# Fused sliding-window attention and MoE block: the last head pair of batches 3 to 7 returned to x^T by the transposing DMA, and seven MoE units in slots 13 to 15

## The chip, the core and the metric

The kernel runs on one core of one Trainium2 chip. The metric is the device time of one execution in microseconds, and smaller is better. Three runs of the kernel before gave 325.88, 325.59 and 325.86 us; their median is 325.86 us.

## The reference: what is computed

Attention over q, k, v of 8 batches, 8 heads, 576 tokens and 64 elements, with a causal window of 128 tokens and a bias that falls linearly with distance (ALiBi). Its output, with the heads side by side, is x of 4608 tokens by 512. Behind it stands a two-layer block with a hard-swish between the layers:

```python
scores = scale * q @ k^T + slope[h] * -(|i - j|)      # only 0 <= i - j < 128
attn   = softmax(scores)
x      = (attn @ v) with heads side by side            # 4608 x 512
h      = x @ w_in                                      # 512 -> 2048
g      = h * clip(h + 3, 0, 6) / 6
out    = g @ w_out                                     # 2048 -> 512, float32
```

## The kernel before, in words

**Tiles.** Attention goes by *head pairs*: pair g holds two heads of batch g // 4, so there are 32 of them, and pairs 3, 7, ..., 31 are the last of their batch. The block goes by tiles nt of 512 tokens, 9 of them. For each tile there are 16 units "U" (`moe_up`: four matmuls of 128x512 over the four 128-row slices ks of x^T, in the order ks = 0 to 3, then a ScalarE activation L470 and a VectorE product L471) and 16 units "D" (`moe_down`: four matmuls of 128x512, L501; after every fourth D, VectorE copies the result (L510) and SyncE sends it out (L511)). Slice ks of x^T is what head pair ks of a batch has put there: the last pair of a batch writes slice 3.

**x^T.** It lies in the tile `xT`, a ring of four batches of 576 columns and 64 columns behind them. `back(g)` (L421) takes the normalized attention output of a pair (`avs`, 128 tokens by 5 groups by 128) and puts its transpose there in one of two ways. Where `by_xbar(g)` (L418) is true, SyncE issues one transposing DMA (L425) of 640 columns. Else TensorE does five 128x128 transposes (L432) into a PSUM bank of the pool that the U units use too, and ScalarE copies 576 columns (L438).

**Order of the work.** From batch 2 on, `segment` (L669) writes out by hand the order of every engine's queue, in slots g = 8 to 32. In slot g come: the scores of pair g (L296, L322, L328), the exps of g on ScalarE and their masks on GpSimd (L351, L354, L361, L364, L367, L370), and, on the results of the slot before, the products with v of pair g - 1 in two halves (`values`: first three groups, then two; L383, L391), each followed by a VectorE reciprocal and product that write `avs` (L401, L402). Between these pieces `fill(n)` puts n MoE units into the queues. The seven numbers `f` say how many go where: `FILLS` gives (1, 1, 1, 2, 0, 1, 1) for slots 9, 10 and 11, which is seven units in a slot, and all others take (1, 1, 1, 2, 0, 1, 2), which is eight. `back(g - 1)` stands behind the second half of `values` where it goes by DMA, and at the slot's end, ahead of its last unit, where it goes by TensorE.

**The order of the units** is one fixed list of 288 (`ORDER`, L513). `fill` stops short where the next unit is a U whose tokens are not all in `xT` yet (L528): `done` counts the pairs that have been put back. With the DMA it rises at the start of the next slot but one (L672), with TensorE at once. What is left of the list when the slots end is put into the queues without a break (`fill(len(units))`, L733); I call that the tail.

**SyncE's queue** is in order. In `stage_next` (L540) it gets, for the batches ahead, the loads of q, k and v (five DMAs each, L112) and the transposing DMAs of q and k (L199) out of one buffer `tbuf`, into which GpSimd casts first q and then k (L194). In slots 16, 20 and 24 `stage_next` comes behind `back` and issues the loads of k and the transposing DMA of q for the next batch; one slot later follow v and the transposing DMA of k. The output DMAs (L511) go through the same queue.

Of the kernel before, what the change touches and what calls it, by code (L numbers as in the profile page):

```python
# [18 lines left out]
def kernel(  # L19
# [16 lines left out]
    NP = H // 2  # L36
# [11 lines left out]
    XB = 2 * NP  # L48
# [367 lines left out]
    done = [0]  # L416

    def by_xbar(g):  # L418
        return g >= XB and g % NP < NP - 1 and g != XB + 2

    def back(g):  # L421
        b, hp = divmod(g, NP)
        avs = st[g, "avs"].rearrange("p j e d -> p j (e d)")
        if by_xbar(g):
            nc.sync.dma_start_transpose(  # L425
                out=xT[:, hp, ds(b % 4 * S, SP)].rearrange("p (j c) -> p j c", j=NQ),
                in_=avs.rearrange("p j c -> p (j c)"))
            return
        pool, tag = (ps_o, "o") if b < 2 else (ps_h, "h")
        tp = pool.tile([128, SP], BF16, tag=tag, name="tb", padded_shape=[128, 1024])  # L430
        for j in range(NQ):
            nc.tensor.transpose(tp[:, ts(j, 128)], avs[:, j, :], ident)  # L432
        if g == NP - 1:
            nc.scalar.copy(out=xT[:, hp, ds(b % 4 * S, 256)], in_=tp[:, 0:256])
            nc.vector.tensor_copy(out=xT[:, hp, ds(b % 4 * S + 256, S - 256)], in_=tp[:, 256:S])
            return
        eng = nc.vector.tensor_copy if g == 2 * NP - 1 else nc.scalar.copy
        eng(out=xT[:, hp, ds(b % 4 * S, S)], in_=tp[:, 0:S])  # L438
# [84 lines left out]
    def fill(n):  # L523
        for _ in range(n):
            if at[0] == len(units):
                return
            nt, fn, step = units[at[0]]
            if fn is moe_up and done[0] < NP * (min((nt * NT + NT - 1) // S, B - 1) + 1):  # L528
                return
            fn(nt if fn is moe_up else nt - 1, step)  # L530
            at[0] += 1
# [132 lines left out]
        scores_diag(2 * NP)  # L664
        scores_off(2 * NP)

    FILLS = {g: (1, 1, 1, 2, 0, 1, 1) for g in (9, 10, 11)}

    def segment(lo, hi, fills):  # L669
        for g in range(lo, hi + 1):  # L670
            f = fills(g)
            if by_xbar(g - 2):  # L672
                done[0] = g - 1
            if lo < g < hi and g != 3 * NP + 1:
                scores(g)
            turn = {2 * NP: (2, 1, "k"), 2 * NP + 1: (2, 1, "q"),
                    2 * NP + 2: (3, 0, "k"), 2 * NP + 3: (3, 1, "k")}.get(g)
            if turn:
                double(*turn, 0, "av", A)
            fill(f[0])  # L680
            if turn:
                double(*turn, 1, *(("h", V) if turn[0] == 2 else ("av", A)))
            if g < hi:
                exp_diag(g, 0)
            fill(f[1])
            if g < hi:
                exp_diag(g, 1)
            if g == 3 * NP:
                cast_tokens(3, "v")
            if g > lo:  # L690
                values(g - 1, (0, 1, 2))
            fill(f[2])
            if g < hi:
                exp_off(g, 0)
            fill(f[3])
            if g < hi:
                exp_off(g, 1)
            if g > lo:
                values(g - 1, (3, 4))
            fill(f[4])  # L700
            if g > lo and by_xbar(g - 1):
                back(g - 1)
            fill(f[5])
            if g < hi:
                stage_next(g)
            fill(1)
            if g == 3 * NP:
                scores(g + 1)
            if g > lo and not by_xbar(g - 1):
                back(g - 1)  # L710
                done[0] = g
            fill(f[6] - 1)
# [3 lines left out]
    with tc.manual_schedule(engines=every):  # L716
# [13 lines left out]
        fill(2)  # L730
        segment(2 * NP, G, lambda g: FILLS.get(g, (1, 1, 1, 2, 0, 1, 2)))
        done[0] = G
# [31 lines left out]
```

## Time and profile before

| what | value |
|---|---|
| median of three runs | 325.86 us |
| span of the profiled execution | 325.3 us |
| TensorE busy | 314.0 us (97%) |
| ScalarE busy | 198.4 us (61%) |
| VectorE busy | 173.7 us (53%) |
| GpSimd busy | 141.4 us (43%) |
| matmuls of U (L451) and D (L501) | 146.2 and 138.6 us |
| transposes of `back` on TensorE (L432) | 75 in 15 pairs |
| transposing DMAs into `xT` (L425) | 17 |

The span runs from the first to the last instruction of the one profiled execution; what lies around it in a run's time is the half microsecond to the median. In a timeline row the first number is the start in us from the span's start and the second the duration; then come the engine, the line, the operation and the tiles, and in brackets the idle time of the engine ahead of it with what ended it. A matmul's duration counts until the model's end of its pipeline, so two that follow each other overlap in the rows; distances from start to start tell more.

### The profile page before, as it was taken

How to read it: one execution, taken by the hardware profiler on the slowest of the kernel's cores; microseconds unless marked ns; L12 is line 12 of the kernel's file. 1: busy time of each engine (PE TensorE's matmuls, PEld its weight loads, DVE VectorE, ACT ScalarE, POOL GpSimd, SP SyncE). 2: the span in 40 equal slices, each digit the busy share in tenths (PEclk: the TensorE clock that was granted, in tenths of full speed). 3: DMA queues.
4: the chain of work that ended last, by engine and by line, in shares of the span. 5: the costliest groups of instructions: out<-in, count | busy, mean ns of one | idle time of the engine just before them, and what ended most of it. 6: DMA issues, size and time to landing. Idle time of an engine off the chain costs nothing.

```text
span 325.3 us, 7087 instructions
## 1 busy us (share of the span) xinstructions
PE 314.0 (97%) x2763; PEld 168.4 (52%) x2763; DVE 173.7 (53%) x338; ACT 198.4 (61%) x339; POOL 141.4 (43%) x249
## 2 busy tenths in 40 slices
PE   7869999999999999999999999999999999999996
PEld 6555465455555555555667655554554444444443
DVE  7657565554445655565555555554565544445510
ACT  4748877877766666666666666666666344244411
POOL 7446393495395566636663666462342000000000
PEclk9999999999999999999999999999999999999999
DMA  7999999799999999799989986931114100000112
GB/s 274 197 328 180 224 298 191 167 257 218 202 254 176 238 212 208 178 222 217 194 146 229 198 207 138 202 107 64 40 36 55 64 33 34 32 32 34 61 41 91
DMA packets 128065, 51.08 MB, mean 157 GB/s; under 512 B 115616, under 2 KB 119968, under 8 KB 128032
## 3 DMA queue, kind: packets, MB, share of 16 engines
q1 hardware_dynamic: 122800, 44.54, 63.4%
q0 software_dynamic: 4224, 4.19, 8.2%
q10 hardware_dynamic: 1008, 1.90, 1.6%
q8 instruction: 21, 0.34, 0.5%
q14 instruction: 12, 0.10, 0.1%
HBM read 36.70 MB, written 9.44 MB: 142 GB/s over the span
## 4 chain that ended last, share of the span: by engine, by line
PE 82%; DMA 7%; ACT 4%; SPq 3%; DVE 1%; issue 1%; POOL 0%; ACTq 0%
PE ops L501 37%; PE hps L451 34%; DMA ldbuf<-in_q_dram 3%; PE scd L296 2%; PE av L391 2%; DMA w_in_sb<-in_moe_w_in_dram 2%; SPq L112 2%; PE av L383 2%; DMA ldbuf<-in_k_dram 2%; ACT r L470 2%; SPq L98 1%; PE sco L328 1%; ACT xT L438 1%; PE ops L482 1%; PE tb L432 1%
## 5 line engine op out<-in xcount | busy, mean ns | idle before, releaser
L471 DVE SCALAR_TENSOR_TENSOR gbuf<-r,hps 128x512 bf16<-128x512 f32 x144 | 98.5, 686 | 104.8 <-ACT r L470 104.8
L470 ACT ACTIVATE r<-hps,bias 128x512 f32<-128x512 f32 x144 | 99.0, 689 | 82.1 <-PE hps L451 81.8
L451 PE MATMUL hps<-xT,w_in_sb 128*128 128x512 bf16 (+1 forms) x640 | 146.2, 358 | 2.7 <-DMA w_in_sb<-in_moe_w_in_dram 1.9
L501 PE MATMUL ops<-w_out_sb,gbuf 128*128 128x512 bf16 x560 | 138.6, 379 | 0.0
L451 PEld LDWEIGHTS <-w_in_sb 128*128 128x128 bf16 x640 | 58.8, 98 | 56.4 <-DMA w_in_sb<-in_moe_w_in_dram 3.0
L501 PEld LDWEIGHTS <-gbuf 128*128 128x128 bf16 x560 | 52.0, 98 | 56.0
L354 POOL TENSOR_SCALAR_AFFINE_SELECT pd<-pd 128x512 bf16<-128x512 bf16 x48 | 30.0, 633 | 58.4 <-ACT pd L351 58.4
L364 POOL TENSOR_SCALAR_AFFINE_SELECT po<-po 128x512 bf16<-128x512 bf16 x48 | 30.3, 634 | 25.5 <-ACT po L361 24.7
L351 ACT ACTIVATE pd<-scd,bias_d 128x512 bf16<-128x512 f32 x48 | 32.1, 685 | 2.6 <-POOL vbuf L187 2.6
L361 ACT ACTIVATE po<-sco,bias_o 128x512 bf16<-128x512 f32 x48 | 33.2, 692 | 0.0
L510 DVE COPY osb<-ops 128x512 f32<-128x512 f32 x33 | 22.7, 688 | 18.7 <-PE ops L501 18.1
L194 POOL CAST tbuf<-ldbuf 128x512 bf16<-128x512 f32 (+1 forms) x45 | 25.6, 611 | 3.9 <-DMA qTb<-tbuf 3.1
L402 DVE TENSOR_TENSOR avs<-av,rc 128x384 bf16<-128x384 f32 (+1 forms) x48 | 23.6, 491 | 1.6
L391 PEld LDWEIGHTS <-pd 128*128 128x128 bf16 x192 | 14.3, 97 | 8.2 <-issue 0.9
L438 ACT COPY xT<-tb 128x576 bf16<-128x576 bf16 x13 | 8.3, 638 | 16.7 <-PE tb L432 16.7
L383 PE MATMUL av<-vbuf,po 128*128 128x65 bf16 x192 | 18.0, 193 | 0.0
L391 PE MATMUL av<-vbuf,pd 128*128 128x65 bf16 x192 | 17.3, 194 | 0.3 <-ACT kTb L244 0.3
L187 POOL CAST vbuf<-ldbuf 128x1024 bf16<-128x1024 f32 x14 | 14.3, 1040 | 5.2 <-DMA ldbuf<-in_v_dram 5.2
L383 PEld LDWEIGHTS <-po 128*128 128x128 bf16 x192 | 14.3, 98 | 3.0 <-DVE avs L402 0.5
L227 POOL CAST pr<-ldbuf 128x576 bf16<-128x576 f32 x20 | 12.8, 668 | 6.6 <-PE tb L432 2.5
L367 ACT ACTIVATE p4buf<-sco,bias_d 128x64 bf16<-128x64 f32 x48 | 15.7, 327 | 0.0
L296 PEld LDWEIGHTS <-kTb 64*128 64x128 bf16 x256 | 7.2, 94 | 14.1 <-issue 10.6
(96 smaller groups left out, 227.3 us busy)
## 6 DMA issues: line engine op xcount, KB each, us to landing
out_dram<-osb SPq DMA_DIRECT2D x33, 256.0 KB, 2.4
ldbuf<-in_v_dram SPq DMA_DIRECT2D x32, 256.0 KB, 5.6
ldbuf<-in_q_dram SPq DMA_DIRECT2D x20, 256.0 KB, 4.7
ldbuf<-in_k_dram SPq DMA_DIRECT2D x16, 256.0 KB, 4.8
ldbuf<-in_q_dram SPq DMA_DIRECT2D x12, 288.0 KB, 7.8
ldbuf<-in_k_dram SPq DMA_DIRECT2D x12, 288.0 KB, 8.1
w_in_sb<-in_moe_w_in_dram POOLq DMA_DIRECT2D x4, 512.0 KB, 9.8
w_out_sb<-in_moe_w_out_dram POOLq DMA_DIRECT2D x4, 512.0 KB, 11.3
```

The lines of the kernel that those rows point to most:

```text
L194: nc.gpsimd.tensor_copy(out=tbuf[:m, :, j, :], in_=s[:m, j, :, :].rearrange("p (i e) d -> p i (e d)", e=2))
L351: nc.scalar.activation(out=pd[:, e, :, :].rearrange("p j c -> p (j c)"), in_=sc[:, e, :], func=ACT.Exp, bias=bias_d[:, h:h + 1], scale=scale)
L354: nc.gpsimd.affine_select(out=pd[:, e, :, :], in_=pd[:, e, :, :], pattern=[[0, 4], [1, 128]], channel_multiplier=-1, base=0, compare_op=AL ...
L361: nc.scalar.activation(out=po[:, e, :, :].rearrange("p j c -> p (j c)"), in_=sc[:, e, :], func=ACT.Exp, bias=bias_o[:, h:h + 1], scale=scale)
L364: nc.gpsimd.affine_select(out=po[:, e, :, :], in_=po[:, e, :, :], pattern=[[0, 4], [-1, 128]], channel_multiplier=1, base=-1, compare_op=A ...
L383: nc.tensor.matmul(out_av, lhsT=po[:, e, qt % 4, :], rhs=vb[:, qt - 1, h, :], start=True, stop=False)
L391: nc.tensor.matmul(out_av, lhsT=d, rhs=vb[:, qt, h, :], start=(qt == 0), stop=True)
L402: nc.vector.tensor_tensor(out=st[g, "avs"][:, qts[0]:qts[0] + nq, :, :], in0=av[:, 0:nq, :, 0:D], in1=rc[:, 0:nq, :, :].to_broadcast([128, ...
L451: nc.tensor.matmul(hps[:, lo:hi], lhsT=w_in_sb[:, ks, ts(ms, 128)], rhs=xT[:, ks, ds(src, hi - lo)], start=(ks == 0), stop=(ks == n_ks - 1))
L470: nc.scalar.activation(out=r6, in_=hps, func=ACT.Relu, bias=bias3[:, 0:1], scale=1.0 / 6.0)
L471: nc.vector.scalar_tensor_tensor(out=gts[nt][:, ms, :], in0=r6, scalar=1.0, in1=hps, op0=ALU.min, op1=ALU.mult)
L501: nc.tensor.matmul(ops[nt, sub], lhsT=gts[nt][:, ms, ts(sub, 128)], rhs=w_out_sb[:, ms, :], start=(ms == 0), stop=(ms == n_ms - 1))
```

## The change

```diff
     def by_xbar(g):
-        return g >= XB and g % NP < NP - 1 and g != XB + 2
+        return g >= XB and g != XB + 2 and g != XB + 3
...
-    FILLS = {g: (1, 1, 1, 2, 0, 1, 1) for g in (9, 10, 11)}
+    FILLS = {g: (1, 1, 1, 2, 0, 1, 1) for g in (9, 10, 11, 13, 14, 15)}
```

XB is 8 and NP is 4. Pairs 15, 19, 23, 27 and 31 now go back by the transposing DMA; pairs 10 and 11 stay on TensorE. Slots 13, 14 and 15 take seven units in place of eight. Nothing else changes in the text of the kernel; the list of units is the same, so each of its units behind slot 13 comes up to three places later against the attention.

## The prediction

> **What bounds the kernel now.** I read the page's first part, the clock row and the shares of the chain that ended last.
>
> ```profile
> PE 314.0 (97%) x2763; PEld 168.4 (52%) x2763; DVE 173.7 (53%) x338; ACT 198.4 (61%) x339; POOL 141.4 (43%) x249
> PEclk9999999999999999999999999999999999999999
> PE 82%; DMA 7%; ACT 4%; SPq 3%; DVE 1%; issue 1%; POOL 0%; ACTq 0%
> ```
>
> TensorE is busy for 97% of the span at its full granted clock, and the chain runs on it for 82%; the DMA's 7% belong to the start. So the next view is busy time by stretches: two ordinary slots of eight units, and most of the tail.
>
> ```profile
> 109.50:117.61 8.11, 8.11 (x71) 4.07 (x70) 4.57 (x10) 6.05 (x11) 3.30 (x6) 1.00 1.09 229
> 126.24:134.36 8.12, 8.12 (x69) 4.07 (x70) 3.97 (x9) 6.15 (x11) 3.84 (x8) 1.00 1.14 196
> 257.00:320.00 63.00, 62.92 (x294) 28.67 (x293) 27.16 (x40) 23.34 (x35) 0.00 (x0) 1.00 0.11 42
> ```
>
> The columns behind the length are TensorE, weight loads, VectorE, ScalarE, GpSimd, clock, DMA share (over 1 here) and GB/s. An ordinary slot is TensorE from end to end, 8.11 us of 8.11; ScalarE has about 2 us to spare. The tail is as dense. What leaves TensorE's queue therefore shortens the time by its own length, as long as nothing else comes late.
>
> Now the slots that hold a `back` on TensorE. This is TensorE's timeline; the L296 rows are the starts of the slots' scores, and the slots are 16 (117.61), 20, 24, 28 and 32.
>
> ```profile
> 117.61 0.40 PE L296 MATMUL scd<-qTb,kTb 64*128 64x128 bf16 x8
> ...
> 122.79 0.19 PE L383 MATMUL av<-vbuf,po 128*128 128x65 bf16 x1
> ...
> 124.76 0.44 PE L432 MATMUL tb<-ident,avs 128*128 128x128 bf16 x5
> 125.04 1.27 PE L451 MATMUL hps<-xT,w_in_sb 128*128 128x512 bf16 x4
> 126.24 0.40 PE L296 MATMUL scd<-qTb,kTb 64*128 64x128 bf16 x8
> ...
> 150.58 0.40 PE L296 MATMUL scd<-qTb,kTb 64*128 64x128 bf16 x8
> ...
> 159.11 0.40 PE L296 MATMUL scd<-qTb,kTb 64*128 64x128 bf16 x8
> ...
> 183.58 0.40 PE L296 MATMUL scd<-qTb,kTb 64*128 64x128 bf16 x8
> ...
> 192.24 0.40 PE L296 MATMUL scd<-qTb,kTb 64*128 64x128 bf16 x8
> ...
> 216.57 0.40 PE L296 MATMUL scd<-qTb,kTb 64*128 64x128 bf16 x8
> ...
> 225.21 0.40 PE L296 MATMUL scd<-qTb,kTb 64*128 64x128 bf16 x8
> ...
> 256.05 0.44 PE L432 MATMUL tb<-ident,avs 128*128 128x128 bf16 x5
> 256.33 2.13 PE L451 MATMUL hps<-xT,w_in_sb 128*128 128x512 bf16 x8
> 258.29 1.03 PE L501 MATMUL ops<-w_out_sb,gbuf 128*128 128x512 bf16 x4
> ```
>
> From scores to scores these slots take 8.63, 8.53, 8.66 and 8.64 us, with eight units each like the ordinary 8.12. The excess is 0.51, 0.41, 0.54 and 0.52 us. It has two parts. The five transposes take 0.28 us (124.76 to 125.04). The U behind them is the first of the next tile, and its last matmul reads the slice that has just been transposed:
>
> ```profile
> 125.24 0.64 ACT L438 COPY xT<-tb 128x576 bf16<-128x576 bf16 x1 [1.73 <-PE tb L432]
> ```
>
> ScalarE's copy ends at 125.88, but the fourth matmul would have been due three quarters of a unit behind 125.04. A unit's length comes from the chain's longest piece:
>
> ```profile
> 308.53 10.36 PE ops L501 x48
> ```
>
> Forty-eight matmuls are twelve units, so 0.863 us each, and the fourth matmul was due at 125.69. So TensorE waits there, which is the rest of the excess, some 0.24 us.
>
> **The change part by part.**
>
> *Five backs leave TensorE and ScalarE.* In slots 16, 20, 24 and 28 the excess goes: 0.51 + 0.41 + 0.54 + 0.52 = 1.98 us. In slot 32 the transposes take 256.33 - 256.05 = 0.28 us, and the two U behind take 258.29 - 256.33 = 1.96 in place of 1.73, another 0.23; together 0.51. In all 2.49 us. The five copies on ScalarE (0.64 each) lie beside TensorE and are worth nothing beyond the wait just counted. The PSUM bank that `tb` took is free for U units; I give that nothing, as no wait for that bank shows in an ordinary slot.
>
> *Three units move to the tail.* Slots 13 to 15 lose 3 x 0.863 = 2.59 us of TensorE work and the tail gets it back: 78 units in place of 75. Both are TensorE from end to end, so the sum is nothing. The cover is that a seven-unit slot stays bound by TensorE: 8.11 - 0.86 = 7.25 us against 6.05 us or less on ScalarE, 4.57 on VectorE and 3.30 on GpSimd in the ordinary slot. If these slots did not shrink at all, the change would cost 2.59 here. Counted through the list, no `fill` from slot 16 on is cut short: the first U of a new tile now falls to the third `fill` of slots 17, 21, 25, 29, where `done` has risen, and in the tail to the third unit. That is what the shift by three units does.
>
> *Five transposing DMAs are added.* Each has to land ahead of the fourth matmul of that U. The time from `avs` and the time to landing:
>
> ```profile
> 123.46 0.42 DVE L402 TENSOR_TENSOR avs<-av,rc 128x256 bf16<-128x256 f32 x1
> ```
>
> ```profile
> DMA to landing us min/median/max: 2.4/2.7/4.9
> ```
>
> The second half of `values` starts at 122.79 and `avs` is complete at 123.88, that is 1.09 us later. TensorE's time from the start of that half to that U in the next slot is five units (three here, two there) and all the attention of a slot, 8.12 - 8 x 0.863 = 1.21 us: 5.53 us, and 0.65 more to its fourth matmul, 6.18. The DMA of the shown 17 needs 1.09 + 2.4 to 4.9 = 3.5 to 6.0 us. In the tail there are five units and the half itself (0.25) ahead, and 0.65: 5.22 against the same 3.5 to 6.0. So at the median (3.8) nothing waits, with 2.4 and 1.4 us in hand; at the longest landing slot 32 would lose 0.8. I take zero, nearest to the median, and keep up to 1 us for the range.
>
> *SyncE waits at a new place.* The added DMA stands ahead of the loads of k in slots 16, 20 and 24, and waits there for `avs`; behind it wait five loads, the transposing DMA of q and the outputs. For them GpSimd's cast of k waits (it needs `tbuf` free), and in the end the scores of the next batch.
>
> ```profile
> 108.28 3.72 SPq L199 DMA_TRANSPOSE kTb<-tbuf  x1
> ...
> 121.92 5.38 SPq L112 DMA_DIRECT2D ldbuf<-in_k_dram  x5
> ...
> 139.30 3.73 SPq L199 DMA_TRANSPOSE kTb<-tbuf  x1
> ...
> 153.47 4.56 SPq L112 DMA_DIRECT2D ldbuf<-in_k_dram  x5
> ...
> 185.93 0.38 SPq L511 DMA_DIRECT2D out_dram<-osb  x1
> 186.36 5.36 SPq L112 DMA_DIRECT2D ldbuf<-in_k_dram  x5
> ```
>
> ```profile
> DMA to landing us min/median/max: 4.9/5.5/7.0
> ```
>
> Capacity first: the twelve groups of issues from 153.47 to 185.93 come to 27.8 us in a period of 32.9 (to 186.36). One more L425 of about 1.24 makes 29.1 of the new 32.4. It fits, with less to spare.
>
> Then the deadlines. Batch 4: k's transposing DMA is issued at 108.28, which the change does not move, and lands at 113.8 (115.3 at the longest). The scores of pair 16 come at 117.61 - 2.59 = 115.0. Batch 5: `avs` of pair 15 is complete at 123.88 - 2.59 = 121.3, SyncE is free at 121.9, so the loads of k start 1.25 us later than before, and k's DMA goes out at 139.30 + 1.25 = 140.6 at the latest, landing at 146.1 (147.6). The scores of pair 20 are due at 150.58 - 2.59 - 0.51 = 147.5. Both hold at the median by over a microsecond and miss by 0.1 to 0.3 at the longest landing. From batch 6 on, SyncE waits for `avs` itself: the loads start at 156.86 - 3.1 + 1.25 = 155.0 in place of 153.47 and end at 159.6; q's DMA lands by 166.6 at the longest, and then GpSimd casts k:
>
> ```profile
> 166.69 2.83 POOL L194 CAST tbuf<-ldbuf 128x512 bf16<-128x512 f32 x5
> 170.24 0.64 POOL L354 TENSOR_SCALAR_AFFINE_SELECT pd<-pd 128x512 bf16<-128x512 bf16 x1 [0.72 <-ACT pd L351]
> ```
>
> The cast then ends at 169.4, and the four large masks of pair 22 behind it (0.6 each) at 171.9. They are needed by the first `values` of slot 23, at 159.11 - 3.5 + 2 x 8.12 + 2.3 = 174.2. It holds by 2 us. I take zero for this step, and up to 1.5 us for the range.
>
> The sum is -2.49 us. The span is 325.3 us and the median of the runs 325.86, half a microsecond around it, so I take the sum from the median: 325.86 - 2.49 = 323.4 us.
>
> **The rivals.**
>
> *The transposing DMA lands behind the U that needs it (slower).* The place is the fourth matmul of the first U of tiles 3 to 7. With a landing of T the loss is 4 x (T + 1.09 - 6.18) + (T + 1.09 - 5.22) = 5 T - 24.5 us; from T = 5.4 us it is more than the 2.49 gained. At T = 7.0, the longest landing of the larger q and k transposes, it is 10.5 us, so 333.9 us. For it speaks that the new DMAs run beside output and load traffic, where the longest of the 17 was measured; against it, that all 17 stay below 5.4. Chance 0.07.
>
> The Trainium skill speaks for this rival: VectorE: DVE Perf Modes, in "The three transpose paths", gives 1309 ns for a 128x128 transpose by DMA against 390 ns on TensorE, and its "Rules for kernel authors" take TensorE where a PSUM destination will do. Taken one after another, five such blocks make 6.5 us by my estimate from that page, and the sum would be 331.6 us. The trace disagrees for this shape: the five blocks land in 2.4 to 4.9 us together, and five on TensorE take 0.28 us of its queue.
>
> *SyncE's queue makes the q and k transposes late (part of the gain lost).* For it: the two margins above that vanish at the longest landings. Against it: even the full shift of the loads (5 us against TensorE's work) meets 5.8 us (batch 5: 139.30 + 5.5 to 150.58) in hand. A loss of 0.3 us up to 0.5 in each of four batches gives 324.4, between 323.7 and 325.4. Chance 0.12.
>
> *The seven-unit slots do not shrink, or a fill runs dry (no change).* The three units then cost 2.59 us in the tail and eat the gain: 325.9 us. For it: SyncE issues without a gap through these slots. Against it: no engine but TensorE is near full in them. Chance 0.07.
>
> **How the numbers follow.** The forecast, 323.4 us with its own range 322.9 to 323.8, has 0.74. The measurement tells 0.2% (0.65 us) from no change, so faster is anything under 325.2. Faster: 0.74 and most of the second rival, 0.84. Same: the third and the rest of the second, 0.08. Slower: 0.08. The range reaches from 322.8, if the two parts of the excess are a little larger than counted, to 324.8, which takes in the bounds of late landing and two thirds of the second rival.
>
> **What would show it.** Right: slots 16, 20, 24 and 28 take 8.1 us from scores to scores, slots 13 to 15 about 7.25, no L432 behind 93 us, 22 DMAs of L425, and TensorE without a wait at the first U of tiles 3 to 7. Wrong: TensorE idle ahead of a U with the DMA into `xT` as releaser; idle ahead of the scores of pairs 16, 20, 24 or 28 with qTb or kTb as releaser; GpSimd's masks behind a longer wait for `tbuf` and `values` waiting for them.

## The result, and the profile after

| | before | after | ratio, 95% interval |
|---|---|---|---|
| first measurement, 4 runs each | 325.87 us | 322.97 us | 0.9918 [0.9903, 0.9932] |
| second, 35 and 12 runs | 325.91 us | 324.26 us | 0.9946 [0.9925, 0.9967] |
| third, 23 and 12 runs | 326.28 us | 323.66 us | 0.9932 [0.9911, 0.9953] |

The changed kernel is faster by 0.5 to 0.8%, that is 1.7 to 2.9 us; 2.5 us were forecast. The three measurements differ by more than such runs should if only the change counted, and the profiles show why: the start of the kernel scatters (below). From the scores in slot 12 on, the traces repeat to a hundredth, so they answer the question of the sum better than the medians.

TensorE's timeline of the changed kernel: the starts of the scores of slots 12 (pair 13), 14, 15, 16, 17, then 20 and 21, 24 and 25, 28 and 29, and between them the U at which the changed kernel could have waited, the first of tile 3.

```profile
90.22 0.40 PE L296 MATMUL scd<-qTb,kTb 64*128 64x128 bf16 x8
...
99.09 0.40 PE L296 MATMUL scd<-qTb,kTb 64*128 64x128 bf16 x8
...
106.34 0.40 PE L296 MATMUL scd<-qTb,kTb 64*128 64x128 bf16 x8
...
113.58 0.40 PE L296 MATMUL scd<-qTb,kTb 64*128 64x128 bf16 x8
...
121.70 0.40 PE L296 MATMUL scd<-qTb,kTb 64*128 64x128 bf16 x8
...
124.30 1.89 PE L451 MATMUL hps<-xT,w_in_sb 128*128 128x512 bf16 x8
126.03 1.03 PE L501 MATMUL ops<-w_out_sb,gbuf 128*128 128x512 bf16 x4
...
146.04 0.40 PE L296 MATMUL scd<-qTb,kTb 64*128 64x128 bf16 x8
...
154.16 0.40 PE L296 MATMUL scd<-qTb,kTb 64*128 64x128 bf16 x8
...
178.63 0.40 PE L296 MATMUL scd<-qTb,kTb 64*128 64x128 bf16 x8
...
186.78 0.40 PE L296 MATMUL scd<-qTb,kTb 64*128 64x128 bf16 x8
...
211.11 0.40 PE L296 MATMUL scd<-qTb,kTb 64*128 64x128 bf16 x8
...
219.23 0.40 PE L296 MATMUL scd<-qTb,kTb 64*128 64x128 bf16 x8
```

The slots that held a transpose took 8.63, 8.53, 8.66 and 8.64 us; they now take 8.12, 8.12, 8.15 and 8.12, the length of any other. Slots 14 and 15 take 7.25 and 7.24, seven units without a gap. The two U at 124.30 end 1.73 us later to the hundredth: no wait for the new DMA. Now the whole stretch, from the scores in slot 12 to the last output's issue; SyncE's timeline, first of before, then of after:

```profile
322.74 0.33 SPq L486 DMA_DIRECT2D out_dram<-osb  x1
```

```profile
318.83 0.33 SPq L486 DMA_DIRECT2D out_dram<-osb  x1
```

Those scores started at 91.64 us before and at 90.22 after. So the stretch took 322.74 - 91.64 = 231.10 us and takes 318.83 - 90.22 = 228.61 us: 2.49 less, which is the predicted sum. A second profile of before gave 322.03 - 90.93 = 231.10, two more of after 321.88 - 93.26 = 228.62 and 318.42 - 89.80 = 228.62.

What SyncE's queue does around the first new DMA, with the time to landing of all 22, and where GpSimd pays for it:

```profile
119.86 0.53 SPq L511 DMA_DIRECT2D out_dram<-osb  x1
120.96 1.20 SPq L425 DMA_TRANSPOSE xT<-avs  x1
122.21 4.49 SPq L112 DMA_DIRECT2D ldbuf<-in_k_dram  x5
126.81 3.76 SPq L199 DMA_TRANSPOSE qTb<-tbuf  x1
...
138.32 3.73 SPq L199 DMA_TRANSPOSE kTb<-tbuf  x1
```

```profile
DMA to landing us min/median/max: 2.4/2.5/4.3
```

```profile
134.17 2.84 POOL L194 CAST tbuf<-ldbuf 128x512 bf16<-128x512 f32 x5 [5.23 <-DMA qTb<-tbuf]
136.96 1.22 POOL L354 TENSOR_SCALAR_AFFINE_SELECT pd<-pd 128x512 bf16<-128x512 bf16 x2
138.14 1.22 POOL L364 TENSOR_SCALAR_AFFINE_SELECT po<-po 128x512 bf16<-128x512 bf16 x2
```

The loads of k now stand behind the wait for `avs`, and GpSimd waits 5.23 us for `tbuf`. Its masks for pair 18 end at 139.36, and the first products that read them start in slot 19 some 2.3 us behind its scores (137.93), at 140.2. The wait is real, and there was room for it. The room is smaller one batch earlier, in slot 15, where pair 14's masks follow the cast of k for batch 4; GpSimd's timeline, then the first TensorE product that reads a mask of L364:

```profile
103.24 2.84 POOL L194 CAST tbuf<-ldbuf 128x512 bf16<-128x512 f32 x5 [3.80 <-DMA qTb<-tbuf]
...
107.22 1.22 POOL L364 TENSOR_SCALAR_AFFINE_SELECT po<-po 128x512 bf16<-128x512 bf16 x2
```

```profile
108.69 0.19 PE L383 MATMUL av<-vbuf,po 128*128 128x65 bf16 x1
```

These masks end at 108.44, so 0.25 us were in hand; the other two profiles of the changed kernel had 2.25 and 0.4. In the kernel before, the same masks ended at 108.9 and were read at 111.85, 3.0 us later. Counted from the scores in slot 12, the shorter slots bring the reader 1.7 us forward, and q's DMA ahead of that cast landed 7.5 us after its issue in this profile (5.2 and 6.9 in the other two, 5.7 before).

### The profile page after: what moved, and what is told of

It reads as the page before. It is cut to its first block, busy times and chain, and to the rows that moved or that the text cites. A ratio compares the mean times of both kernels' runs of the same rounds, so it can differ in the third digit from the quotient of the medians.

```text
span 321.6 us, 7050 instructions
## 1 busy us (share of the span) xinstructions
PE 312.4 (97%) x2738; PEld 167.6 (52%) x2738; DVE 173.0 (54%) x338; ACT 195.6 (61%) x334; POOL 141.1 (44%) x249
## 4 chain that ended last, share of the span: by engine, by line
PE 82%; DMA 10%; SPq 2%; POOL 2%; DVE 1%; ACT 1%; issue 1%; POOLq 0%
PE ops L501 37%; PE hps L451 33%; DMA w_out_sb<-in_moe_w_out_dram 5%; DMA ldbuf<-in_v_dram 3%; PE scd L296 3%; DMA ldbuf<-in_k_dram 2%; PE av L391 2%; SPq L112 2%; PE av L383 2%; PE sco L328 1%; PE ops L482 1%; PE w L153 1%; POOL w_out_sb L171 1%; PE tp L219 0%; ACT kTb L244 0%
## 5 line engine op out<-in xcount | busy, mean ns | idle before, releaser
L471 DVE SCALAR_TENSOR_TENSOR gbuf<-r,hps 128x512 bf16<-128x512 f32 x144 | 98.7, 687 | 102.5 <-ACT r L470 100.2
L364 POOL TENSOR_SCALAR_AFFINE_SELECT po<-po 128x512 bf16<-128x512 bf16 x48 | 30.3, 636 | 32.5 <-ACT po L361 32.3
L391 PE MATMUL av<-vbuf,pd 128*128 128x65 bf16 x192 | 17.3, 194 | 0.3 <-ACT kTb L244 0.3
L296 PE MATMUL scd<-qTb,kTb 64*128 64x128 bf16 x256 | 12.7, 219 | 1.7 <-DVE kTb L220 0.9
```

What stands on the lines that cost most here:

```text
L296: nc.tensor.matmul(scd[:, e, ts(j, 128)], lhsT=kT[r, j, :], rhs=qT[r, j, :], start=first, stop=first or j == 3)
L364: nc.gpsimd.affine_select(out=po[:, e, :, :], in_=po[:, e, :, :], pattern=[[0, 4], [-1, 128]], channel_multiplier=1, base=-1, compare_op=A ...
L391: nc.tensor.matmul(out_av, lhsT=d, rhs=vb[:, qt, h, :], start=(qt == 0), stop=True)
L471: nc.vector.scalar_tensor_tensor(out=gts[nt][:, ms, :], in0=r6, scalar=1.0, in1=hps, op0=ALU.min, op1=ALU.mult)
```

## The experiments

My theory at this point: the gain is time that leaves TensorE's queue (five transposes and five waits for ScalarE's copy); the moved units are neutral; the DMAs land in time. Rivals: the shift of the units does the work, the landing or SyncE's queue takes part of the gain back, or the change moves the start of the kernel. "Stretch" is the time from the scores in slot 12 to the last output's issue (231.10 before, 228.61 after), taken from each run's trace.

### The five DMAs alone

```diff
-    FILLS = {g: (1, 1, 1, 2, 0, 1, 1) for g in (9, 10, 11, 13, 14, 15)}
+    FILLS = {g: (1, 1, 1, 2, 0, 1, 1) for g in (9, 10, 11)}
```

> The five DMAs alone: slots 13 to 15 keep eight units. Theory (the gain is TensorE's queue time, 5 x 0.28 us of transposes and 5 x 0.23 us of waits for ScalarE's copy; the new DMAs land 2.4 to 2.6 us after their issue): the first U of tile 3 now stands first in slot 17, behind one unit less in slot 16, and its fourth matmul is due 3.3 us behind the second half of values, against 1.09 + 2.4 to 2.6 = 3.5 to 3.7 for the DMA; in slots 21, 25 and 29 it is due after 4.1, in the tail after 3.5. So at most 0.6 us is lost against the changed kernel: 323.0 to 323.6 us. Rival (the landing is what the three moved units are there to cover, at up to 4.9 us): waits of 2.7 + 3 x 1.9 + 2.5 = 10.9 us, up to 333.9 us.

Measured: 325.01 us, 0.9965 [0.9945, 0.9984] of before, where 323.0 to 323.6 was expected; the changed kernel beside it took 324.26. Its stretch is 319.67 - 90.08 = 229.59 us, so 0.98 more than with the shift; 0.6 at most was expected. TensorE's timeline at the first U of tile 3:

```profile
123.29 0.40 PE L296 MATMUL scd<-qTb,kTb 64*128 64x128 bf16 x8
...
123.84 0.82 PE L451 MATMUL hps<-xT,w_in_sb 128*128 128x512 bf16 x3
124.89 1.24 PE L451 MATMUL hps<-xT,w_in_sb 128*128 128x512 bf16 x5 [0.23 <-DMA xT<-avs]
```

Three matmuls run, then the fourth waits for the DMA into its slice, as the theory says; that slot takes 8.50 us in place of 8.12. Slots 25 and 29 take 8.32 and 8.21, and the first two U of tile 7 take 2.02 us in place of 1.73. I had nothing for the two slots and 0.2 us at most for tile 7. For these three, `avs` was complete 1.8, 1.8 and 1.3 us behind the start of the second half of `values`, where I took 1.09 from one slot of the kernel before. So the landing is a real deadline, the DMAs bring 1.5 us by themselves, and three moved units are what buys the last 1.0.

### The seven-unit slots alone

```diff
-    FILLS = {g: (1, 1, 1, 2, 0, 1, 1) for g in (9, 10, 11)}
+    FILLS = {g: (1, 1, 1, 2, 0, 1, 1) for g in (9, 10, 11, 13, 14, 15)}
```

(in the kernel before)

> The seven-unit slots alone: all five last pairs stay on TensorE. Theory: moving three units costs nothing, but the unit behind the transposes is now a D, so the 0.23 us that the first U waited for ScalarE's copy go five times: 325.87 - 1.15 = 324.7 us, with the five transposes of 0.28 us still there. If the wait were only hidden by the DMA and not by the order of units, or if the transposes were the whole excess: 325.9. If the slots did not shrink: 325.9 + 2.6 - 1.15 = 327.3.

Measured: 325.40 us, 0.998 [0.9961, 0.9998]; stretch 320.13 - 89.69 = 230.44, which is 0.66 less than before and not 1.15. TensorE's timeline at the transposes of slot 16:

```profile
119.36 1.03 PE L501 MATMUL ops<-w_out_sb,gbuf 128*128 128x512 bf16 x4
120.22 0.53 PE L432 MATMUL tb<-ident,avs 128*128 128x128 bf16 x5
120.59 1.03 PE L501 MATMUL ops<-w_out_sb,gbuf 128*128 128x512 bf16 x4
121.55 0.40 PE L296 MATMUL scd<-qTb,kTb 64*128 64x128 bf16 x8
```

Behind the transposes stands a D that waits for no copy, and still it starts 0.37 us after them, not 0.28. The excess of the slot is 8.49 - 8.12 = 0.37. VectorE's timeline of this run, then TensorE's weight loads for the transposes in the kernel before and in this run (a transpose loads its 128x128 of `avs` as weights), and the last two loads of this run alone:

```profile
119.17 0.69 DVE L471 SCALAR_TENSOR_TENSOR gbuf<-r,hps 128x512 bf16<-128x512 f32 x1 [0.89 <-ACT r L470]
...
119.98 0.42 DVE L402 TENSOR_TENSOR avs<-av,rc 128x256 bf16<-128x256 f32 x1
```

```profile
124.55 0.48 PEld L432 LDWEIGHTS <-avs 128*128 128x128 bf16 x5
```

```profile
120.01 0.57 PEld L432 LDWEIGHTS <-avs 128*128 128x128 bf16 x5
```

```profile
120.46 0.11 PEld L432 LDWEIGHTS <-avs 128*128 128x128 bf16 x2
```

The five loads take 0.09 us longer, and that is a new wait. The fourth transpose is the first that reads the second half of `avs`. Here this half is complete at 120.41, behind the start of the transposes, and the fourth load starts at 120.46; in the kernel before it was complete at 123.88, 0.9 us ahead of the transposes. The three moved units put a U in place of a D just ahead of the second half of `values`, and VectorE makes that U's product (L471, to 119.86) before it turns to `avs`. So this run takes the waits for the copy away and puts five smaller waits for `avs` in.

### The transposes kept, without use

```diff
+            elif g > lo and g % NP == 0:
+                avs = st[g - 1, "avs"].rearrange("p j e d -> p j (e d)")
+                tp = ps_h.tile([128, SP], BF16, tag="h", name="tb", padded_shape=[128, 1024])
+                for j in range(NQ):
+                    nc.tensor.transpose(tp[:, ts(j, 128)], avs[:, j, :], ident)
```

(in the changed kernel, where `back` by TensorE stood)

> The changed kernel, and beside the five DMAs the five transposes of the last pairs on TensorE as before, at the same place, but with no copy and no reader: work that is left without use, to price the transposes alone. Theory: 5 x 0.28 = 1.4 us more than the changed kernel, 324.4 us, and no wait at the U behind them. If the PSUM bank they take makes U units wait: more than 1.4. If TensorE had room for them: 323.0.

Measured: 325.63 us, 0.9985 [0.9968, 1.0002] of before; stretch 320.92 - 90.47 = 230.45, so 1.84 us more than the changed kernel: five times 0.37, where five times 0.28 was expected. TensorE had no room for them. TensorE's weight loads in slot 16:

```profile
120.79 0.57 PEld L716 LDWEIGHTS <-avs 128*128 128x128 bf16 x5
```

They take 0.57 us as in the run before it, with the same wait of the fourth for `avs` (complete at 121.19, loaded at 121.24), so with 5 x 0.28 = 1.4 us and some 0.4 of such waits nothing is left for a wait for the PSUM bank. The two runs agree from both sides: 0.66 by the order of units and 1.84 by the transposes are 2.50, the whole of the gain. The waits for `avs` make the first number smaller and the second larger by as much.

### The DMA behind the loads of k

```diff
-            if g > lo and by_xbar(g - 1):
+            if g > lo and by_xbar(g - 1) and g % NP:
                 back(g - 1)
             fill(f[5])
             if g < hi:
                 stage_next(g)
+            if g > lo and by_xbar(g - 1) and g % NP == 0:
+                back(g - 1)
             fill(1)
```

> The changed kernel with the last pair's DMA issued behind the loads of k and the transposing DMA of q in slots 16, 20 and 24 (in 28 and 32 nothing stands ahead of it), so that SyncE does not wait for avs ahead of the loads. Theory of the deadline: in slot 16 SyncE is free at 121.0, the loads take 4.5 to 5.4 us and q's DMA 3.8, so the DMA into xT goes out near 130.3 and lands near 132.9, against the fourth matmul of the first U of tile 3 due near 125.0: a wait of 6 to 8 us, three times, so 18 to 24 us: 341 to 347 us. TensorE idle at that U with the DMA into xT as releaser. Rival (the order on SyncE matters little, or the loads that come earlier give time back): under 330.

Measured: 348.19 us, 1.0674 [1.0644, 1.0705], above the 341 to 347 expected. TensorE's timeline at the first U of tile 3, and the stretch of slot 17 cut in five (TensorE busy is the second number, the clock the third from the end):

```profile
130.98 2.29 PE L451 MATMUL hps<-xT,w_in_sb 128*128 128x512 bf16 x5 [6.46 <-DMA xT<-avs]
```

```profile
121.11:124.50 3.39, 3.23 (x39) 1.87 (x40) 0.90 (x4) 1.26 (x2) 3.39 (x7) 1.00 1.18 244
124.52:129.18 4.66, 0.00 (x1) 0.00 (x0) 0.47 (x1) 0.00 (x0) 0.03 (x1) 1.00 1.36 215
129.22:130.98 1.76, 0.00 (x0) 0.00 (x0) 0.00 (x0) 0.00 (x0) 0.00 (x0) 0.50 0.65 155
130.98:136.05 5.07, 5.07 (x19) 2.06 (x19) 1.93 (x4) 2.94 (x6) 2.04 (x5) 0.50 0.11 43
136.05:138.32 2.27, 2.27 (x13) 0.89 (x11) 0.73 (x2) 0.69 (x1) 2.25 (x5) 1.00 0.32 72
```

The mechanism of the prediction's slower rival is there where it was put. Its price was too low: the slot grew by 17.21 - 8.12 = 9.1 us, of which 6.5 are the wait. The rest is the clock: it falls to 0.50 while TensorE idles, and when TensorE starts again it stays there for 5.1 us, which costs half of them. Three such slots (17, 21 and 25: waits of 17.3 us together) cost the stretch 343.95 - 89.62 - 228.61 = 25.7 us. So a late landing costs about 1.5 times its wait here, once the wait is this long. The Trainium skill, in TensorE: Matmul & The Clock Gate, "The HAM clock gate (the "warmup" mystery)", has the gate fall to half rate after an idle window of about 3.4 us and come back after a busy one of that length, and the window is free-running. This run agrees on the half rate. The fall came 4.7 us into the idling and the return 5.1 us into the work; both are longer than one window, which a free-running window allows.

### Pair 10 by the DMA too

```diff
-        return g >= XB and g != XB + 2 and g != XB + 3
+        return g >= XB and g != XB + 3
```

> The changed kernel with pair 10 back by the DMA too (pair 11 stays). Theory: in slot 11 five more transposes leave TensorE, 0.28 us, at most 0.37 with the gap up to the scores behind them, and the first U that needs pair 10 comes a slot later: 322.6 to 322.7 us. Rival (SyncE's queue is full around slot 12 and the added issue makes q and k late): 323.0 or more.

Measured: 323.78 us, 0.9938 [0.9917, 0.9959] of before; 322.6 to 322.7 was expected. Slot 11 is 0.29 us shorter (8.21 for 8.50), as expected, but slot 13 is 0.79 longer (9.66 for 8.87). SyncE's timeline, then TensorE's:

```profile
82.58 4.17 SPq L112 DMA_DIRECT2D ldbuf<-in_q_dram  x5
86.85 0.56 SPq L511 DMA_DIRECT2D out_dram<-osb  x1
87.50 1.91 SPq L425 DMA_TRANSPOSE xT<-avs  x1
```

```profile
91.90 1.46 PE L451 MATMUL hps<-xT,w_in_sb 128*128 128x512 bf16 x6 [0.86 <-DMA xT<-avs]
```

`avs` of pair 10 was complete at 84.38, but SyncE was busy issuing loads; the DMA went out at 87.50, landed at 91.9, and the first U of tile 2 waited 0.86 us. By the trace that loses 0.5 us in all, where I expected a gain of 0.3 (from the scores in slot 9 to the last output's issue 257.57 us, and 257.10 in the changed kernel); the medians can't tell it from the changed kernel. It is not the rival either: TensorE waited nowhere for q or k, but for the added DMA itself. My expectation had the next U "a slot later", but slot 12, whose fills are cut short, takes only 4.0 us.

### Pair 10 by the DMA, and the loads of q behind it

```diff
-    LOADS = {9: "v3", 10: "q4", 12: "k4", 13: "v4", 14: "q5", 16: "k5", 17: "v5", 18: "q6",
+    LOADS = {9: "v3", 11: "q4", 12: "k4", 13: "v4", 14: "q5", 16: "k5", 17: "v5", 18: "q6",
```

(on top of the run before)

> Pair 10 back by the DMA as in the run that did so alone, and the loads of q for batch 4 moved one slot later, behind that DMA on SyncE. In the run with pair 10 alone the DMA of pair 10 stood behind those loads (82.58 to 86.75) and an output, went out at 87.50 though avs was complete at 84.4, landed 4.4 us later, and TensorE waited 0.86 us for it at the first U of tile 2. Theory: with the loads behind it the DMA goes out near 84.5 and that wait goes, so from the scores of slot 9 to the last output the trace shows 257.1 - 0.3 = 256.8 us, 0.3 less than the changed kernel; the time 0.3 us under that of the changed kernel on the same chip, which the scatter of the start may hide. Rival (the loads of q are now late for GpSimd's cast, and with them the scores of pair 16): a wait ahead of the scores of pair 16 and 257.5 us or more.

Measured: 325.28 us, 0.9973 [0.9957, 0.999] of before, slower than the changed kernel beside it on the same chip (323.66, 0.9932 [0.9911, 0.9953]). The wait at tile 2 is gone (slot 13 takes 8.87 again), and the rival's delay came, though at another place: no wait ahead of the scores of pair 16, but one for masks in slot 15. From the scores in slot 9 it takes 258.75 us; 256.8 was expected, 257.5 or more by the rival. GpSimd's timeline, then TensorE's in slot 15:

```profile
106.15 2.83 POOL L194 CAST tbuf<-ldbuf 128x512 bf16<-128x512 f32 x5 [6.01 <-issue]
```

```profile
107.04 0.40 PE L296 MATMUL scd<-qTb,kTb 64*128 64x128 bf16 x8
...
110.21 0.20 PE L391 MATMUL av<-vbuf,pd 128*128 128x65 bf16 x1 [0.38 <-POOL pd L354]
110.79 0.20 PE L383 MATMUL av<-vbuf,po 128*128 128x65 bf16 x1 [0.38 <-POOL po L364]
...
116.22 0.40 PE L296 MATMUL scd<-qTb,kTb 64*128 64x128 bf16 x8
```

The later loads move q's DMA of batch 4 by 2.9 us: it is issued 99.19 - 90.92 = 8.3 us behind the scores in slot 12, and 95.62 - 90.22 = 5.4 in the changed kernel. GpSimd's cast of k behind it waits for `tbuf` for 6.01 us (the timeline names no releaser; q's DMA lands 6.8 us behind its issue, at 106.0), the masks of pair 14 behind the cast come late, and TensorE waits for them. Slot 15 takes 9.18 us in place of 7.24. Counted from the scores in slot 12, the cast of k starts 2.2 us later than in the changed kernel (106.15 - 90.92 against 103.24 - 90.22), and of these the 0.25 us of room in slot 15 are free: 1.94 us are lost. This is the second rival of the prediction, made to happen.

### The two kernels once more

> The changed kernel once more, for a second profile and a narrower interval. If the gain is what the trace shows from slot 12 on, 2.5 us, and the rest of the measured 2.9 is the scatter of the start: between 2.5 and 2.9 faster, and a start (up to the scores in slot 12) that differs between two profiles of the same kernel by some tenths of a microsecond. If the change itself shortens the start: the same start as in the first profile.

> The kernel before once more, for a second profile of its start. If the start scatters from one execution to the next, its profile differs from the first one's in the time up to the scores in slot 12 (91.64 us from the span's start, 92.2 with what lies around the span) by some tenths of a microsecond; if not, the same. Time 325.9.

> The changed kernel a third time, beside the run above on one chip. Theory: from the scores of slot 12 to the last output 228.6 us as in both profiles so far; the start ends anywhere between 89 and 93 us, with the kernel before too; faster by 1.7 to 2.9 us.

Measured: the ratios of the second and third row of the first table, and before against itself 325.89 to 325.89 us (1.0005 [0.9991, 1.0019]). The stretches are those given above. The starts end at 91.64 and 90.93 in the two profiles of before and at 90.22, 93.26 and 89.80 in the three of after, and in the four other runs that are the same up to there at 89.62 to 90.47. So the start scatters by over 3 us, not by some tenths as expected, and I see no sign that it follows the kernel: with 2.49 us taken off, the three differences of the medians leave 0.41, -0.84 and 0.13 us. The second measurement's 1.65 us lies below the 2.5 to 2.9 expected for it. TensorE's timeline of the 93.26 one, then its stretch behind that row, and the part of it at the lower clock:

```profile
36.35 1.26 PE L451 MATMUL hps<-xT,w_in_sb 128*128 128x512 bf16 x4 [2.03 <-DMA w_in_sb<-in_moe_w_in_dram]
```

```profile
37.54:42.80 5.26, 5.26 (x36) 2.30 (x36) 1.42 (x3) 4.18 (x6) 2.79 (x5) 0.72 1.05 352
```

```profile
37.03:40.44 3.41, 3.41 (x17) 1.34 (x16) 0.69 (x1) 2.28 (x4) 0.43 (x1) 0.50 1.05 310
```

There is a wait of 2.03 us for the weights; 0.7 us after work has begun again, the granted clock falls to 0.50 for 3.41 us. In the 90.22 one the same 36 TensorE records take 3.90 us at full clock. The first before waited 0.80 us there.

## Why the prediction was right

**The sum.** Slots 16, 20, 24 and 28: 1.98 us predicted, 0.51 + 0.41 + 0.51 + 0.52 = 1.95 measured. Slots 13 to 15: 2.59 predicted to leave, 0.88 + 0.85 + 0.88 = 2.61 measured (9.75 to 8.87, 8.10 to 7.25, 8.12 to 7.24). From the scores in slot 29 to the last output: 2.59 - 0.51 = 2.08 more predicted, 99.60 - 97.53 = 2.07 measured. In all 2.49 and 2.49. The last hundredths are luck: 0.03 too much in the first term (the slots beside slot 24 take 8.15 and not 8.12) and 0.02 too little in the second cancel.

**The split inside an excess held.** I put 0.28 us on the transposes and 0.24 on the wait for ScalarE's copy. The two runs that take one without the other give 0.37 and 0.13 on the average, but in both of them, and not in the kernel before, the transposes wait 0.09 us for `avs`. With this wait taken out, the rows of the kernel before close the sum: five times 0.28 for the transposes, four times 0.24 for the copy, and 0.41 - 0.28 = 0.13 in slot 20, are 2.49. So nothing is left for the PSUM bank or the copies, which I had put at nothing. Both expectations, 1.15 and 1.4 us, were off because I took the order of the work around the transposes to be unchanged.

**The landing.** The DMA went out as soon as `avs` was complete (120.93, issue 120.96) and landed 2.6 us later at 123.6; the fourth matmul was due at 124.30 + 0.65 = 124.95, so 1.4 us were in hand (2.4 predicted at the median). In the tail the DMA landed at 252.70 and the fourth matmul was due at 252.66 + 0.65 = 253.31, so 0.6 us were in hand (1.4 predicted). The term that was off is the time to `avs`: 1.09 us behind the start of the second half of `values` in the prediction, 2.16 in all five slots here, by the U's product that now stands ahead on VectorE. The five new DMAs landed in 2.4 to 2.6 us, below the 2.7 that I took, and that covered part of it. That the three moved units are needed for it was argued from counted fills; the run without them shows it, at 1.0 us.

**SyncE's queue.** The start was 1.42 us shorter in this profile, so I count from the scores in slot 12. The loads of k were predicted at 121.92 + 1.25 - 91.64 = 31.5 us and went out at 122.21 - 90.22 = 32.0, later because `avs` was; k's DMA for batch 5 went out at 48.1 (48.9 at the latest predicted). GpSimd's wait for `tbuf` was predicted, but I worked out its room for batch 6 alone (2 us); in batch 5 it is 0.9 us. For batch 4 I looked at k's DMA and not at the masks behind the cast, and the room there, 0.25 us in slot 15, was narrower still. That it cost nothing was luck; the sum had no term for it.

**The time.** The forecast of 323.4 us lies 0.1% over the first median and under the other two. What I did not see is that the profile of before was, it seems, of a slower execution: in every later run the time is 1.7 us above the span, and not half a microsecond, so 325.3 us of span should stand for about 327.0 and not for the median. As only the difference of the stretch was used, the forecast is untouched. The slower rival's price (5 T - 24.5) left the clock out.

## What to carry to other kernels

Where one engine is busy from end to end, read the price of a step from the distance between two marks of the slots with it and without it, and not from the step's own rows: the total came out to 0.01 us. When a run is to price one part alone, look whether it puts another wait in the place of what it takes away: 0.09 us for `avs` made a right price look wrong here. Moving work from the full engine to a DMA pays as long as the DMA lands ahead of its reader, and a few units of other work moved between them can see to that. They brought 1.0 us here, but they also made `avs` 1.07 us later and took 1.7 of the 3.0 us of room from the masks in slot 15. Before anything is put into or moved within an in-order queue that is nearly full, follow each thing behind it to its deadline: the loads behind the new DMA went out 1.7 us later for nothing, and 2.2 us of delay to a cast one batch earlier cost 1.9.

## What the runs showed of the hardware

- In TensorE's waits of 6.46, 5.04 and 5.79 us the granted clock was 1.00 for the first 4.7, 4.0 and 4.4 us and then 0.50, up to 5.1, 5.8 and 5.5 us after work had begun again. A wait of 2.03 us in one start was followed, 0.7 us into the work, by 3.41 us at 0.50; a wait of 1.72 us in another run was followed by none.
- Five transposes of 128x128 with a unit behind them took 0.28 us of TensorE's time where their input was ready, and 0.36 to 0.37 where the fourth waited for it.
- A transposing DMA of 640 columns landed 2.4 us after its issue at the least, and up to 5.1 us after it.
- The same kernel's start ended between 89.8 and 93.3 us in three executions.
